# Attention ahead of two MLPs: the order of the work set step by step on four engines

## The chip, the cores and the metric

The kernel runs on one core of a Trainium2 chip. The metric is the device time of one execution in microseconds. The kernel before was run three times on its own and once under the hardware profiler. "Span" is the profiled stretch from its first to its last instruction, and all positions below ("at 33.67") are microseconds from its start.

## The reference

A soft-capped attention over 2 batches and 12 heads (448 tokens, 64 columns per head) feeds a relu-squared MLP, and that feeds a SoLU MLP. The change touches the first part and its seam to the second.

```python
def _attn_ref(q, k, v, cap):
    scale = 1.0 / np.sqrt(q.shape[-1])
    scores = scale * np.matmul(q, k.transpose(0, 1, 3, 2))
    scores = cap * np.tanh(scores / cap)
    scores = scores - np.max(scores, axis=-1, keepdims=True)
    attn = np.exp(scores)
    attn = attn / (np.sum(attn, axis=-1, keepdims=True) + 1e-09)
    return np.matmul(attn, v).astype(np.float32)

x = attn_out.transpose(0, 2, 1, 3).reshape(896, 768)
h = x @ w_in                       # 768 x 2048
r = np.maximum(h, 0.0)
y = (s * (r * r) + b) @ w_out      # then the SoLU MLP on y
```

## The kernel before

**Tiling.** The attention works on twelve head pairs, called n = 0 to 11 here; a pair is two heads of one batch. Products of full precision are made of three matmuls over split operands (a high and a low part: `kh`, `kl`, `qh`, `ql`, `xh`, `xl`). The maximum is not searched for, since the cap bounds the scores. An input-dependent branch chooses between two arms; the arm that runs here is the one without `general`, whose tiles are laid out by key.

**The steps of a pair.**

- `prep(n)`: TensorE (PE) transposes k and q into the PSUM tiles `pk` and `pq` (L412). VectorE (DVE) makes `kh`, `kl` and `ql` (L431, L432, L424), ScalarE (ACT) makes `qh` (L423).
- `scores_by_key(n, c)`, c = 0 to 3: PE writes a score tile `s` (L450), ACT reads it with a tanh into the tile `e` (L455). Two score tiles exist, so a score step waits for the tanh of the step before the last.
- `exps_by_key(n)`: ACT takes the exponential of `e` in two halves (L462). GpSimd (POOL) adds the tiles of `e` into `c` in two steps (L467, L468, 2.1 us each), and DVE closes the sum with two short instructions (L471).
- `products_by_key(n, half)`: PE multiplies `e` with v into the PSUM tile `o`, eight matmuls each half (L483).
- `values_by_key(n)`: PE spreads the sums into the PSUM tile `m` (L497). DVE turns that (`mt`, L504), takes the reciprocal (`few`, L506), spreads it (`rs`, L510) and scales `o` to `xf` (L515). POOL splits `xf` into `xh` and `xl` (L520, L524).

The PSUM tiles `pk`, `pq`, `o` and `m` of all pairs share four slots. A slot can be written again when its reader is done: `kl` for `pk`, `ql` for `pq`, `xf` for `o`, `mt` for `m`.

**The order.** The loop below is the whole attention. `on_pe` fixes only the order on PE: each step comes behind the last PE instruction of the step ahead. The order on DVE, ACT and POOL is the scheduler's. Iteration n runs scores of pair n, products and sums of pair n-2 and prep of pair n+2. The first half of the products stands between score steps 1 and 2, the second half behind step 3.

**The weights.** The first MLP's weight blocks `wi0`, `wi1`, ... arrive as 64-bit numbers in two raw tiles and are converted in seven operations (`convert`, L218 to 250: ACT L223, DVE L224, L228, L233, L237, ACT L243, DVE L244). `weights.pump(1)` runs one step of that; before, one step stands behind each pair from iteration 3 on, and a raw tile is loaded again when its block is converted. MLP matmuls of block `wi0` (L327 to L329, tile `in`) start on PE while the last pair's products are still to be done.

**The start.** Fourteen small matmuls on `ones` (L169, tile `idle`) run ahead of everything on PE. POOL's queue holds the loads of q for three groups, memsets of the unused parts of each loaded tile, three small loads (`s_t`, `b_t`, `g_t`, L160) and the identity matrix. On DVE four tiny operations on `b_t` (L742, L743) stand ahead of the first `kh`.

Of the kernel before, what the change touches and what calls it, by code (L numbers as in the profile page):

```python
# [37 lines left out]
def tile_softcap_attention__relu2__solu(  # L38
# [50 lines left out]

    def load_by_key(t, src, b, heads, by_pair=False, odd=None):  # L90

        n_heads = heads.stop - heads.start
        for par in range(2):
            fours, threes = (slice(0, D), slice(D, P))[::1 - 2 * par]
            lo = 4 * D if par == 0 else 3 * D
            toks = (slice(0, lo), slice(lo, S))[::1 - 2 * par]
            queue = odd if odd and par else nc.sync
            for rows, tok, n in ((fours, toks[0], 4), (threes, toks[1], 3)):  # L100
                part = src[b, heads.start + par:heads.stop:2, tok]
                if by_pair:
                    for pr in range(n_heads // 2):
                        queue.dma_start(
                            out=t[rows, pr, :n, par],
                            in_=part[pr].rearrange("(p c) d -> p c d", c=n),
                        )
# [5 lines left out]
            if by_pair:  # L113
                nc.gpsimd.memset(t[threes, :, 3:, par], 0.0)
            else:
                nc.gpsimd.memset(t[threes, par:n_heads:2, 3 * D:], 0.0)
            yield
# [15 lines left out]
    nc.scalar.dma_start(out=cap_t, in_=cap.partition_broadcast(P))  # L133
    load_by_query(first["q"][:, 1:], q, 0, slice(2, 4), nc.gpsimd)
    for pr in range(2):
        pair = slice(2 * pr, 2 * pr + 2)
        odd = nc.scalar if pr == 0 else nc.sync
        for _ in load_by_key(first["k"][:, pr:pr + 1], k, 0, pair, by_pair=True, odd=odd):
            pass
# [6 lines left out]
    ident = cst.tile([P, P], F32, name="ident")  # L146
    make_identity(nc, ident)
# [8 lines left out]
    for t, src in (  # L156
        (s_t, s_in.partition_broadcast(P)), (b_t, b_in.partition_broadcast(P)),
        (g_t, g_ln.rearrange("(k p) -> p k", p=P)),
    ):
        nc.gpsimd.dma_start(out=t, in_=src)  # L160
# [5 lines left out]
    with psum("ps_w", 1) as ps_w:  # L166
        idle = ps_w.tile([P, 512], F32, name="idle")
        for n in range(14):
            nc.tensor.matmul(idle[:D, :D], lhsT=ones, rhs=ones, start=True, stop=True)  # L169
# [14 lines left out]
    def layers(ctx, general):  # L184
# [33 lines left out]
        def convert(wt, raw, n, h, l, g=None):  # L218
# [4 lines left out]
            nc.scalar.activation(out=w, in_=hi.bitcast(F32), func=AF.Abs)  # L223
# [18 lines left out]
            if g is None:  # L242
                nc.scalar.copy(out=h, in_=w)  # L243
# [8 lines left out]
        class Weights:  # L252
# [31 lines left out]
            def job(self, n):  # L284
                self.load(n + 1)
                name, _, dst, g, _ = self.jobs[n]
                h, l = dst()
                raw, cnt = self.raw.pop(n)
                yield from convert(self.wt_of(f"wt_{name}"), raw, cnt, h, l, g)
                self.parts[name] = h, l  # L290
                self.done += 1
# [82 lines left out]
        nat = {}  # L374

        def load_group(g, names=("k", "q", "v")):
            b, i = divmod(g, GB)
            heads = slice(4 * i, 4 * i + 4)
            for nm, src in (("k", k), ("q", q), ("v", v)):
# [7 lines left out]
                shape = [P, 2, NC, 2, D] if by_pair else [P, 4, NC * D]  # L387
                t = ap_.tile(shape, F32, tag=f"{nm}n", name=f"{nm}n{g}", bufs=3)
                if by_key:
                    for _ in load_by_key(t, src, b, heads, by_pair):  # L390
                        pass
                elif by_pair:
# [10 lines left out]
        def prep(n):  # L403
# [3 lines left out]
            for nm in ("k", "q"):  # L407
# [3 lines left out]
                for c in range(NC):  # L411
                    turn = nc.tensor.transpose(  # L412
# [3 lines left out]
                st["pe"] = turn  # L416
# [5 lines left out]
                if nm == "q":  # L422
                    nc.scalar.mul(out=hi, in_=ps, mul=sc_t)  # L423
# [19 lines left out]
        def scores_by_key(n, c):  # L443
# [4 lines left out]
            for x, (kk, qq) in enumerate(terms(n)):  # L448
                for j, rows in enumerate(both):
                    st["pe"] = nc.tensor.matmul(  # L450
# [4 lines left out]
            st["act"] = nc.scalar.activation(  # L455
# [3 lines left out]
        def exps_by_key(n):  # L459
            e = st["e", n]  # L460
            for tiles in (slice(0, 4), slice(4, 7)):
                nc.scalar.activation(  # L462
                    out=e[:, tiles, :], in_=e[:, tiles, :], func=AF.Exp, scale=a_t, bias=a_t
                )
            c = ap_.tile([P, 2, S], F32, tag="c", name=f"c{n}", bufs=2)
            st["c", n] = c
            nc.gpsimd.tensor_tensor(out=c, in0=e[:, 0:2, :], in1=e[:, 2:4, :], op=ALU.add)  # L467
# [8 lines left out]
        def products_by_key(n, half):  # L476
# [4 lines left out]
            for c in (2 * half, 2 * half + 1):  # L481
                for j in range(2):
                    st["pe"] = nc.tensor.matmul(  # L483
# [6 lines left out]
        def values_by_key(n):  # L490
            b, i_p = divmod(n, NPAIR)
            if n == 0:
                xs["x"] = act_tiles("x")
            tok = slice(b * S, (b + 1) * S)
            m = ps_t.tile([P, 512], F32, tag="t", name=f"m{n}")
            for j in range(2):
                st["pe"] = nc.tensor.matmul(  # L497
# [17 lines left out]
            st["dve"] = nc.vector.tensor_tensor(  # L515
                out=xf, in0=st["o", n][:, :S], in1=r, op=ALU.mult
            )
# [147 lines left out]

        def g_tile(fc, name):
# [7 lines left out]
        load_group(2, ("k", "q"))  # L674
        load_group(1, ("v",))
# [27 lines left out]
        else:  # L703
            def on_pe(step, *args):

                with tc.issue_after(st["pe"].ins):
                    step(*args)

            prep_half(1)
            prep_half(1)  # L710
            weights.load(1)
            load_group(2, ("v",))
            for n in range(NPR + 2):
                now, last = n < NPR, n >= 2
                for c in range(NC):
                    if now:
                        on_pe(scores_by_key, n, c)
                    if c == 1:
                        if 0 <= n - 1 < NPR:
                            exps_by_key(n - 1)  # L720
                        if last:
                            on_pe(products_by_key, n - 2, 0)
                if last:
                    on_pe(products_by_key, n - 2, 1)
                on_pe(prep_half, n + 2)
                on_pe(prep_half, n + 2)
                if last:
                    on_pe(values_by_key, n - 2)
                    with tc.issue_after(st["dve"].ins), tc.issue_after(st["act"].ins):
                        weights.pump((n > 2) if now else 3)  # L730
                if n % 2 == 1 and n // 2 + 3 < NG:
                    load_group(n // 2 + 3)
# [3 lines left out]
        for n in range(GSB):  # L736
# [3 lines left out]
            if n % 2 == 0:  # L740
                behind = slice(M0, M0 + 2)
                nc.vector.tensor_copy(gh[:, behind], b_t.to_broadcast([P, 2]))  # L742
                nc.vector.tensor_tensor(  # L743
                    out=gl[:, behind], in0=b_t.to_broadcast([P, 2]), in1=full(gh[:, behind]),
# [299 lines left out]
```

## Time and profile before

| what | value |
|---|---|
| three runs | 476.80, 477.12, 477.62 us; median 477.12 us |
| the profiled execution | 478.09 us, of which its span is 476.3 us |
| PE busy | 463.2 us, 97% of the span |
| DVE, ACT, POOL busy | 351.8, 275.9, 95.6 us |
| the chain that ended last | PE 95% |
| attention on PE | from 6.31 us; first MLP matmul at 109.15 us |
| one pair in the steady part | 8.22 us, at positions 33.67, 41.89, ..., 91.21 |

The profiled execution is 1.79 us longer than its span and 0.97 us longer than the median of the three runs. A row of a timeline gives start, busy time, engine, line, operation, tile written <- tiles read, and, in brackets, how long the engine sat idle ahead of it and what ended that. Neighbours in a PE timeline overlap (a matmul's end is modelled), so the price of a step is the distance of its start from the start of the next step, not the busy time.

### The profile page before, as it was taken

What the parts mean: (1) busy time and instruction counts of PE and PEld (TensorE: products, weight loads), DVE (VectorE), ACT (ScalarE), POOL (GpSimd) and SP (SyncE); (2) the same over time, 40 slices, a digit from 0 to 9 for tenths busy, and PEclk for the clock granted to TensorE, in tenths of its full rate; (3) what the DMA queues carried; (4) which work ended last, traced back from release to release, by engine and by line L of the source; (5) the groups of instructions that cost most, each with busy time, mean ns of one, the idle gap of its engine ahead of it and who ended that gap; (6) DMA issues with size and microseconds to landing.
All of it is one profiled execution on the core that took longest, in us unless ns stands there. A gap on an engine that the chain in (4) does not pass through costs nothing.

```text
span 476.3 us, 6578 instructions
## 1 busy us (share of the span) xinstructions
PE 463.2 (97%) x2412; PEld 376.9 (79%) x2412; DVE 351.8 (74%) x566; ACT 275.9 (58%) x398; POOL 95.6 (20%) x103
## 2 busy tenths in 40 slices
PE   6799999999999999999999999999999999999995
PEld 5554544445998998988988889989888898999894
DVE  3358999999888899996699988998958984043110
ACT  2989788881666678775677746555625452033120
POOL 8648788894000000000000000000001010000000
PEclk9889999999999999999999999999999999999998
DMA  6885514001546577643223324443311300011112
GB/s 141 162 217 117 129 29 106 0 1 40 194 140 201 180 221 218 198 134 88 61 78 112 105 89 133 131 126 142 135 66 67 132 1 23 11 33 34 34 41 66
DMA packets 43416, 49.28 MB, mean 103 GB/s; under 512 B 20016, under 2 KB 35504, under 8 KB 43376
## 3 DMA queue, kind: packets, MB, share of 16 engines
q1 hardware_dynamic: 41712, 47.39, 34.2%
q0 software_dynamic: 576, 1.15, 1.1%
q8 instruction: 21, 0.34, 0.3%
q10 hardware_dynamic: 1088, 0.23, 0.2%
q14 instruction: 19, 0.16, 0.1%
HBM read 46.01 MB, written 2.75 MB: 102 GB/s over the span
## 4 chain that ended last, share of the span: by engine, by line
PE 95%; ACT 2%; DMA 2%; DVE 0%; SPq 0%; issue 0%
PE in L328 8%; PE o L483 8%; PE in L327 8%; PE y L329 8%; PE y L328 8%; PE y L327 8%; PE in L329 8%; PE s L450 7%; PE h L914 4%; PE h L918 4%; PE h L922 4%; PE o L964 4%; PE o L965 4%; PE o L963 4%; PE m L497 2%; DMA raw<-in_k_dram 2%
## 5 line engine op out<-in xcount | busy, mean ns | idle before, releaser
L328 PE MATMUL in<-xl,h_wi 128*128 128x510 f32 (+2 forms) x192 | 70.0, 365 | 0.0
L327 PE MATMUL in<-xh,h_wi 128*128 128x510 f32 (+2 forms) x192 | 69.8, 365 | 0.0
L329 PE MATMUL in<-xh,l_wi 128*128 128x510 f32 (+2 forms) x192 | 69.6, 364 | 0.0
L899 POOL TENSOR_SCALAR va<-vs 128x1 f32<-128x1 f32 x7 | 2.0, 286 | 321.3 <-ACT e L898 321.3
L359 ACT ACTIVATE gh<-g,s_t 128x510 fp32r<-128x510 f32 (+1 forms) x64 | 42.2, 668 | 19.0 <-PE y L329 19.0
L360 DVE SCALAR_TENSOR_TENSOR gl<-g,s_t,gh 128x510 fp32r<-128x510 f32 (+1 forms) x64 | 42.8, 682 | 3.1 <-ACT gh L359 3.0
L455 ACT ACTIVATE e<-s 128x896 f32<-128x896 f32 (+1 forms) x48 | 36.6, 813 | 8.9 <-PE s L450 6.0
L462 ACT ACTIVATE e<-e,a_t 128x1792 f32<-128x1792 f32 (+1 forms) x24 | 40.8, 1698 | 0.6
L483 PE MATMUL o<-e,vn 128*64 128x448 f32 x192 | 40.9, 550 | 0.0
L328 PEld LDWEIGHTS in<-xl,h_wi 128*128 128x128 f32 x192 | 36.0, 188 | 5.0 <-issue 1.4
L327 PEld LDWEIGHTS in<-xh,h_wi 128*128 128x128 f32 x192 | 36.0, 188 | 4.3 <-issue 0.7
L329 PEld LDWEIGHTS in<-xh,l_wi 128*128 128x128 f32 x192 | 36.0, 188 | 3.6
L963 PE MATMUL o<-w2o_h,lh 128*128 128x384 f32 (+1 forms) x104 | 35.6, 342 | 0.5 <-ACT lh L205 0.5
L965 PE MATMUL o<-w2o_h,ll 128*128 128x384 f32 (+1 forms) x104 | 35.4, 342 | 0.0
L964 PE MATMUL o<-w2o_l,lh 128*128 128x384 f32 (+1 forms) x104 | 35.4, 340 | 0.0
L914 PE MATMUL h<-w2i_h,yh 128*128 128x512 f32 x84 | 33.0, 393 | 0.0
L918 PE MATMUL h<-w2i_l,yh 128*128 128x512 f32 x84 | 33.0, 392 | 0.0
L922 PE MATMUL h<-w2i_h,yl 128*128 128x512 f32 x84 | 32.8, 390 | 0.0
L471 DVE SCALAR_TENSOR_TENSOR c<-c,e 64x448 f32<-64x448 f32 x24 | 26.5, 1102 | 7.2 <-POOL c L468 6.8
L467 POOL TENSOR_TENSOR c<-e 128x896 f32<-128x896 f32 x12 | 25.3, 2108 | 17.4 <-PE m L497 8.7
L205 ACT CAST lh<-x 128x512 fp32r<-128x512 f32 x14 | 7.5, 590 | 35.7 <-PE o L964 35.6
L223 ACT ACTIVATE wt_wi<-raw 128x768 f32<-128x768 f32 x16 | 14.6, 912 | 22.7 <-DMA raw<-in_moe_w_in_dram 12.7
(424 smaller groups left out, 1120.7 us busy)
## 6 DMA issues: line engine op xcount, KB each, us to landing
raw<-in_moe_w_in_dram SPq DMA_DIRECT2D x16, 768.0 KB, 4.9
raw<-in_moe_w_out_dram SPq DMA_DIRECT2D x24, 512.0 KB, 3.6
raw_w2i<-in_moe_w_in_dram SPq DMA_DIRECT2D x12, 512.0 KB, 4.8
raw<-in_moe_w_out_dram SPq DMA_DIRECT2D x8, 768.0 KB, 4.2
vn<-in_v_dram SPq DMA_DIRECT2D x12, 128.0 KB, 3.7
qn<-in_q_dram SPq DMA_DIRECT2D x12, 112.0 KB, 2.8
kn<-in_k_dram SPq DMA_DIRECT2D x20, 64.0 KB, 3.0
vn<-in_v_dram SPq DMA_DIRECT2D x12, 96.0 KB, 3.4
```

The costliest lines, as they stand in the source:

```text
L327: nc.tensor.matmul(o, lhsT=wh, rhs=xh, start=first, stop=False)
L328: nc.tensor.matmul(o, lhsT=wh, rhs=xl, start=False, stop=False)
L329: nc.tensor.matmul(o, lhsT=wl, rhs=xh, start=False, stop=last)
L359: nc.scalar.mul(out=gh[:, :m], in_=r2, mul=s_t)
L360: nc.vector.scalar_tensor_tensor(out=gl[:, :m], in0=r2, scalar=s_t, in1=full(gh[:, :m]), op0=ALU.mult, op1=ALU.subtract,)
L483: st["pe"] = nc.tensor.matmul(o[j * D:(j + 1) * D, :S], lhsT=vn[:, 2 * (n % 2) + j, c * D:(c + 1) * D], rhs=st["e", n][:, 2 * c + j if c < ...
L914: nc.tensor.matmul(ps[:, n, :], lhsT=yh[:, kk, :], rhs=big["w2i_h"][:, kk, f], start=(kk == 0), stop=False,)
L918: nc.tensor.matmul(ps[:, n, :], lhsT=yh[:, kk, :], rhs=big["w2i_l"][:, kk, f], start=False, stop=False,)
L922: nc.tensor.matmul(ps[:, n, :], lhsT=yl[:, kk, :], rhs=big["w2i_h"][:, kk, f], start=False, stop=(kk == KD - 1),)
L963: nc.tensor.matmul(o, lhsT=lh[:, f, :], rhs=wh, start=(f == 0), stop=False)
L964: nc.tensor.matmul(o, lhsT=lh[:, f, :], rhs=wl, start=False, stop=False)
L965: nc.tensor.matmul(o, lhsT=ll[:, f, :], rhs=wh, start=False, stop=(f == KF2 - 1))
```

## The change

The order is now fixed on PE, DVE, ACT and POOL: `then` puts each step's first instruction on each engine behind that engine's last instruction of the steps ahead. The per-pair order is new, and so is the placing of the steps around it:

- iteration n: score steps 0 and 1 of pair n, both halves of the products of n-2, the sums of n-2, score steps 2 and 3, prep of n+2. The x split runs a pair later (`split_x(n-3)`).
- the exponential and the POOL sum of the first half of pair n stand ahead of score step 2; there are three `c` tiles instead of two.
- no conversion step in iterations 3 to 9. `wi0` is converted wholly on DVE: four DVE operations in iteration 1 and three in iteration 2. Iterations 10 to 13 hold 2, 3, 2 and 2 steps of the next blocks.
- `qh` of pairs 1 to 3 is made on DVE. Prep of pair 1 comes behind score steps 0 and 1 of pair 0.
- at the start: 18 matmuls on `ones` ahead of the branch and 6 more behind `pq0`; the identity is made ahead of the q loads; the three small loads come behind the q loads of group 2; the memsets are done once for each of three kept tiles per name; the operations on `b_t` are POOL's.

The core of the diff:

```diff
-        def exps_by_key(n):
+        def exps_by_key(n, half):
             e = st["e", n]
+            tiles = (slice(0, 4), slice(4, 7))[half]
+            nc.scalar.activation(
+                out=e[:, tiles, :], in_=e[:, tiles, :], func=AF.Exp, scale=a_t, bias=a_t
+            )
+
+        def sums_by_key(n, half):
+            e = st["e", n]
+            if half == 0:
+                c = ap_.tile([P, 2, S], F32, tag="c", name=f"c{n}", bufs=3)
+                st["c", n] = c
+                nc.gpsimd.tensor_tensor(out=c, in0=e[:, 0:2, :], in1=e[:, 2:4, :], op=ALU.add)
+                return
+            c = st["c", n]
             nc.gpsimd.tensor_tensor(out=c, in0=c, in1=e[:, 4:6, :], op=ALU.add)
...
-                nc.scalar.activation(out=w, in_=hi.bitcast(F32), func=AF.Abs)
+            if early:
+                nc.vector.tensor_scalar(
+                    out=wb, in0=hi, scalar1=0x7FFFFFFF, scalar2=None, op0=ALU.bitwise_and
+                )
+            else:
+                nc.scalar.activation(out=w, in_=hi.bitcast(F32), func=AF.Abs)
...
-            def on_pe(step, *args):
-                with tc.issue_after(st["pe"].ins):
+            def then(step, *args):
+                with ExitStack() as behind:
+                    for ins in last.values():
+                        behind.enter_context(tc.issue_after(ins))
+                    n = len(traced)
                     step(*args)
+                for ins in traced[n:]:
+                    if ins.engine in ordered:
+                        last[ins.engine] = ins
+            for n in range(6):
+                nc.tensor.matmul(idle[:D, :D], lhsT=ones, rhs=ones, start=True, stop=True)
+            then(scores_by_key, 0, 0)
+            then(scores_by_key, 0, 1)
+            then(prep_half, 1)
+            then(prep_half, 1)
+            weights.load(0)
+            load_group(2, ("k", "q"))
+            load_small()
...
+            steps = {1: 3, 2: 2, NPR - 2: 2, NPR - 1: 3}
             for n in range(NPR + 2):
+                now = n < NPR
+                if now and n > 0:
+                    then(scores_by_key, n, 0)
+                    then(scores_by_key, n, 1)
+                if not now:
+                    then(weights.pump, 2)
+                if n >= 2:
+                    then(products_by_key, n - 2, 0)
+                    then(products_by_key, n - 2, 1)
+                    then(values_by_key, n - 2)
+                if now:
+                    then(exps_by_key, n, 0)
+                if n >= NPR:
+                    then(split_x, n - 2)
+                elif n >= 3:
+                    then(split_x, n - 3)
+                if now:
+                    then(sums_by_key, n, 0)
+                    then(scores_by_key, n, 2)
+                    then(scores_by_key, n, 3)
+                    then(exps_by_key, n, 1)
+                then(prep_half, n + 2)
+                then(prep_half, n + 2)
+                then(weights.pump, steps.get(n, 0))
+                if now:
+                    then(sums_by_key, n, 1)
```

On PE, iteration 3 from its second score step on. The number behind a letter is the pair (`s3_1` is score step 1 of pair 3), the last number only tells tiles apart. Before:

```order
L450 MATMUL s3_1_451<-qh3_336,kl3_328 128x448 x2
L483 MATMUL o1_466<-e1_285,vn0_180 64x448 x4
L450 MATMUL s3_2_471<-qh3_336,kh3_327 128x448 x2
L450 MATMUL s3_2_471<-ql3_337,kh3_327 128x448 x2
L450 MATMUL s3_2_471<-qh3_336,kl3_328 128x448 x2
L450 MATMUL s3_3_479<-qh3_336,kh3_327 128x448
L450 MATMUL s3_3_479<-ql3_337,kh3_327 128x448
L450 MATMUL s3_3_479<-qh3_336,kl3_328 128x448
L483 MATMUL o1_466<-e1_285,vn0_180 64x448 x4
L412 MATMUL pk5_488<-ident_78,kn2_187 128x128 x4
L412 MATMUL pq5_497<-ident_78,qn2_198 128x112 x4
L497 MATMUL m1_506<-c1_382,ones_90 64x448 x2
```

The same place on PE now:

```order
L468 MATMUL s3_1_468<-qh3_351,kl3_343 128x448 x2
L507 MATMUL o1_476<-e1_303,vn0_179 64x448 x8
L517 MATMUL m1_485<-c1_321,ones_88 64x448 x2
L468 MATMUL s3_2_501<-qh3_351,kh3_342 128x448 x2
L468 MATMUL s3_2_501<-ql3_352,kh3_342 128x448 x2
L468 MATMUL s3_2_501<-qh3_351,kl3_343 128x448 x2
L468 MATMUL s3_3_509<-qh3_351,kh3_342 128x448
L468 MATMUL s3_3_509<-ql3_352,kh3_342 128x448
L468 MATMUL s3_3_509<-qh3_351,kl3_343 128x448
L426 MATMUL pk5_515<-ident_62,kn2_231 128x128 x4
L426 MATMUL pq5_524<-ident_62,qn2_242 128x112 x4
```

The products are one piece, and the sums `m1` moved from behind the prep to right behind the products. In the program as built, `o1` is written into the slot that `m0` held, so it waits for `mt0`; `o2` waits for `mt1` in the same way.

On DVE, from the end of pair 3's prep to `xf0`. Before:

```order
L424 SCALAR_TENSOR_TENSOR ql3_337<-pq3_331,sc_t_87,qh3_336 128x448
L471 SCALAR_TENSOR_TENSOR c1_382<-c1_382,e1_285 64x448 x2
L431 CAST kh4_414<-pk4_409 128x512
L432 TENSOR_TENSOR kl4_415<-pk4_409,kh4_414 128x512
L504 STREAM_TRANSPOSE mt0_432<-m0_429 128x448
L424 SCALAR_TENSOR_TENSOR ql4_424<-pq4_418,sc_t_87,qh4_423 128x448
L506 RECIPROCAL few0_434<-mt0_432 128x14
L510 STREAM_TRANSPOSE rs0_436<-few0_434 128x448
L515 TENSOR_TENSOR xf0_438<-o0_387,rs0_436 128x448
```

The same stretch on DVE now:

```order
L442 SCALAR_TENSOR_TENSOR ql3_352<-pq3_346,sc_t_85,qh3_351 128x448
L222 TENSOR_SCALAR wt_wi0_357<-raw0_58 128x768
L227 TENSOR_SCALAR wt_wi0_357<-wt_wi0_357 128x768
L231 TENSOR_SCALAR wt_wi0_357<-wt_wi0_357 128x768
L236 SCALAR_TENSOR_TENSOR wt_wi0_357<-raw0_58,wt_wi0_357 128x768
L495 SCALAR_TENSOR_TENSOR c1_321<-c1_321,e1_303 64x448 x2
L524 STREAM_TRANSPOSE mt0_410<-m0_407 128x448
L526 RECIPROCAL few0_412<-mt0_410 128x14
L530 STREAM_TRANSPOSE rs0_414<-few0_412 128x448
L535 TENSOR_TENSOR xf0_416<-o0_398,rs0_414 128x448
```

Four operations of the conversion of `wi0` now stand ahead of the closing of `c1` and of `mt0`. A pair later the same happens with three:

```order
L442 SCALAR_TENSOR_TENSOR ql4_450<-pq4_444,sc_t_85,qh4_449 128x448
L240 SCALAR_TENSOR_TENSOR wt_wi0_357<-raw0_58,wt_wi0_357 128x768
L247 CAST h_wi0_355<-wt_wi0_357 128x768
L250 TENSOR_TENSOR l_wi0_356<-wt_wi0_357,h_wi0_355 128x768
L495 SCALAR_TENSOR_TENSOR c2_419<-c2_419,e2_381 64x448 x2
L524 STREAM_TRANSPOSE mt1_488<-m1_485 128x448
```

From iteration 3 on DVE's list holds no conversion until iteration 10.

## Rows read from the trace of the kernel before

**Rows 1.** The page's head: busy time, share of the span and instructions by engine.

```profile
PE 463.2 (97%) x2412; PEld 376.9 (79%) x2412; DVE 351.8 (74%) x566; ACT 275.9 (58%) x398; POOL 95.6 (20%) x103
```

**Rows 2.** Windows: stretch, length, busy PE PEld DVE ACT POOL, granted clock, DMA, GB/s.

```profile
20.00:26.00 6.00, 5.71 (x23) 4.50 (x25) 3.27 (x6) 5.32 (x7) 3.62 (x4) 0.50 0.57 149
...
40.00:110.00 70.00, 70.00 (x414) 33.87 (x413) 67.63 (x82) 58.69 (x60) 58.72 (x44) 1.00 0.23 56
```

**Rows 3.** Timeline of PE, from pair 0's first score to pair 3's.

```profile
10.96 0.74 PE L450 MATMUL s<-qh,kh 64*128 64x448 f32 x2
...
13.46 0.47 PE L450 MATMUL s<-qh,kh 64*128 64x448 f32 x2 [0.24 <-ACT e L455]
...
14.97 0.60 PE L412 MATMUL pk<-ident,kn 128*128 128x128 f32 x4
...
16.98 0.47 PE L450 MATMUL s<-qh,kh 64*128 64x448 f32 x2 [1.03 <-ACT e L455]
...
20.29 0.74 PE L450 MATMUL s<-qh,kh 64*128 64x448 f32 x2 [1.81 <-ACT e L455]
...
33.67 0.48 PE L450 MATMUL s<-qh,kh 64*128 64x448 f32 x2
```

**Rows 4.** Timeline of PE, one steady pair: the first row of each step.

```profile
58.33 0.48 PE L450 MATMUL s<-qh,kh 64*128 64x448 f32 x2
...
59.77 1.72 PE L483 MATMUL o<-e,vn 128*64 128x448 f32 x8
61.42 0.47 PE L450 MATMUL s<-qh,kh 64*128 64x448 f32 x2
...
63.02 1.72 PE L483 MATMUL o<-e,vn 128*64 128x448 f32 x8
64.68 0.66 PE L412 MATMUL pk<-ident,kn 128*128 128x128 f32 x4
...
65.65 0.97 PE L497 MATMUL m<-c,ones 128*64 128x448 f32 x4
66.55 0.48 PE L450 MATMUL s<-qh,kh 64*128 64x448 f32 x2
```

**Rows 5.** Timeline of PE at the seam to the MLP.

```profile
105.29 3.18 PE L483 MATMUL o<-e,vn 128*64 128x448 f32 x16
108.30 0.92 PE L497 MATMUL m<-c,ones 128*64 128x448 f32 x4
109.15 0.47 PE L327 MATMUL in<-xh,h_wi 128*128 128x448 f32 x1
```

**Rows 6.** Timeline of ACT, pair 0 and the first tanh of pair 1.

```profile
12.49 1.73 ACT L455 ACTIVATE e<-s 128x896 f32<-128x896 f32 x2 [0.79 <-PE s L450]
...
18.82 0.61 ACT L423 ACTIVATE qh<-pq,sc_t 128x448 fp32r<-128x448 f32 x1
19.33 1.71 ACT L455 ACTIVATE e<-s 128x896 f32<-128x896 f32 x2
```

**Rows 7.** Timeline of DVE: start, a closing sum alone, a `mt`, two conversions.

```profile
8.71 0.24 DVE L742 CAST gh<-b_t 128x2 fp32r<-128x2 f32 x2 [4.81 <-DMA b_t<-in_moe_b_dram]
...
21.17 1.27 DVE L471 SCALAR_TENSOR_TENSOR c<-c,e 64x448 f32<-64x448 f32 x2 [1.02 <-POOL c L468]
...
42.07 0.64 DVE L504 STREAM_TRANSPOSE mt<-m 128x448 f32<-128x448 f32 x1
...
44.68 2.23 DVE L224 TENSOR_SCALAR wt_wi<-wt_wi 128x768 f32<-128x768 f32 x1
...
114.83 0.95 DVE L237 SCALAR_TENSOR_TENSOR wt_wi<-raw,wt_wi 128x768 uint32<-128x768 uint32 x1
...
119.80 0.55 DVE L224 TENSOR_SCALAR wt_wi<-wt_wi 128x768 f32<-128x768 f32 x1
```

**Rows 8.** Timeline of POOL: the two sums of pair 3.

```profile
42.17 2.12 POOL L467 TENSOR_TENSOR c<-e 128x896 f32<-128x896 f32 x1 [0.94 <-PE m L497]
44.37 2.12 POOL L468 TENSOR_TENSOR c<-c,e 128x896 f32<-128x896 f32 x1
```

More of the change, by code (lines that the diff above doesn't have):

```diff
@@ L137, in tile_softcap_attention__relu2__solu @@
         odd = nc.scalar if pr == 0 else nc.sync
-        for _ in load_by_key(first["k"][:, pr:pr + 1], k, 0, pair, by_pair=True, odd=odd):
-            pass
+        load_by_key(first["k"][:, pr:pr + 1], k, 0, pair, by_pair=True, odd=odd)
         if pr == 0:
@@ L167, in tile_softcap_attention__relu2__solu @@
         idle = ps_w.tile([P, 512], F32, name="idle")
-        for n in range(14):
+        for n in range(18):
             nc.tensor.matmul(idle[:D, :D], lhsT=ones, rhs=ones, start=True, stop=True)
@@ L288, in job @@
                 raw, cnt = self.raw.pop(n)
-                yield from convert(self.wt_of(f"wt_{name}"), raw, cnt, h, l, g)
+                yield from convert(
+                    self.wt_of(f"wt_{name}"), raw, cnt, h, l, g, name == "wi0" and not general
+                )
                 self.parts[name] = h, l
@@ L374, in layers @@
         nat = {}
+        kept = {}
         def load_group(g, names=("k", "q", "v")):
@@ L422, in prep @@
                 if nm == "q":
-                    nc.scalar.mul(out=hi, in_=ps, mul=sc_t)
+                    if n in (1, 2, 3) and not general:
+                        nc.vector.tensor_scalar(
+                            out=hi, in0=ps, scalar1=sc_t, scalar2=None, op0=ALU.mult
+                        )
+                    else:
+                        nc.scalar.mul(out=hi, in_=ps, mul=sc_t)
                     nc.vector.scalar_tensor_tensor(
@@ L664, in layers, with load_small @@
             add_w2out(f)
+        def load_small():
+            for t, src in (
+                (s_t, s_in.partition_broadcast(P)), (b_t, b_in.partition_broadcast(P)),
+                (g_t, g_ln.rearrange("(k p) -> p k", p=P)),
+            ):
+                nc.gpsimd.dma_start(out=t, in_=src)
         def g_tile(fc, name):
@@ new lines, in layers @@
+            ordered = [e.engine for e in (nc.tensor, nc.vector, nc.scalar, nc.gpsimd)]
+            xs["x"] = act_tiles("x")
+            idle = ps_t.tile([P, 512], F32, tag="t", name="idle2")
+            for n in range(6):
[5 more added lines that the diff above has]
+            weights.load(0)
+            load_group(2, ("k", "q"))
@@ L711, in layers @@
+            load_small()
+            load_group(1, ("v",))
+            load_group(2, ("v",))
             weights.load(1)
-            load_group(2, ("v",))
+            steps = {1: 3, 2: 2, NPR - 2: 2, NPR - 1: 3}
             for n in range(NPR + 2):
[L714 to L730, printed above, removed]
+                now = n < NPR
[24 more added lines that the diff above has]
+                    then(sums_by_key, n, 1)
+                if n == NPR - 1:
+                    then(split_x, n - 2)
@@ L740, in layers @@
             if n % 2 == 0:
[L741 to L744, printed above, removed]
+                ends = slice(M0, M0 + 2)
+                nc.gpsimd.tensor_copy(gh[:, ends], b_t.to_broadcast([P, 2]))
+                nc.gpsimd.tensor_tensor(
+                    out=gl[:, ends], in0=b_t.to_broadcast([P, 2]), in1=full(gh[:, ends]),
                     op=ALU.subtract,
```

86 lines of the change are left out of this document (43 added, 43 removed).

## The prediction

> **What bounds the kernel now.** I read the page's head first: PE is busy 97% of the span [rows 1]. The windows then say where it is not, or is slow: from 40 to 110 PE has 70.00 of 70.00 us at a granted clock of 1.00, and from 20 to 26 it is busy 5.71 of 6.00 at 0.50, the 1.2 GHz level of its two (1.2 and 2.4) [rows 2]. So after the start only less time per matmul can help, and at the start there is idle time and a low clock to win. The timeline of PE shows the start: it waits for a tanh for 0.24, 1.03 and 1.81 us, and the stretch at half clock comes right behind the last two waits [rows 3]. In the same table of windows DVE stands at 67.63 of 70, next to full, and POOL at 58.72 [rows 2]. That fits the view of single rows: a conversion that takes 0.55 alone took 2.23 at 44.68, ending just behind a POOL sum that ran from 44.37 to 46.49 [rows 7, 8]. So a DVE operation of this kind and a POOL sum do not run at once: the later one waits for the whole of the earlier. Since this is where my forecast is decided, the Trainium skill is weighed on it further down.
>
> **Part 1: a steady pair.** The new order makes the same matmuls, with fewer changes between kinds. Step by step before, by distances of starts [rows 4]: scores 0 and 1 1.44 (58.33 to 59.77), half a product 1.65, scores 2 and 3 1.60, the other half 1.66, prep 0.97, sums 0.90; together 8.22. Now: scores 1.44; both halves in one piece 3.01 (105.29 to 108.30 is such a piece, [rows 5]); sums behind products 0.85 [rows 5]; scores 2 and 3 with a prep behind them 1.51 (13.46 to 14.97, [rows 3]); prep 0.97. Sum 7.78, a gain of 0.44 per pair. Were only the products' joint won, it would be 0.30; 0.50 if the prep also shrinks to the 0.92 that the changes of kind around it leave room for by my estimate. Seven pairs (3 to 9) have no other load: 7 x 0.44 = 3.1 (2.1 to 3.5). Pairs 10 and 11 have no prep and conversions again: 0.4 together (0 to 0.9). What must keep up: ACT takes 6.84 per pair (12.49 to 19.33, [rows 6]), so 0.94 of 7.78 is its cover; POOL has two sums of 2.2 and a split, 58.72 of 70 us for 8.5 pairs, 6.9 per pair, so its cover is 0.9; DVE loses its conversion, up to 2.23 a pair, so its cover grows. I take nothing for these; if one is late, the pair falls back to 7.8 to 8.2, which is in the bounds. The split a pair later only matters for when `xf` comes free, at no cost.
>
> **Part 2: the start.** Before, DVE stood 4.81 us on the load of `b_t` until 8.71 and made `kh0` behind that [rows 7]; now nothing stands ahead of `kh0`, and prep of pair 1 stands behind the first two score steps. I estimate the first score about 1.0 earlier than 10.96 [rows 3]. Then ACT: of its 6.84 per pair 0.51 is `qh` (18.82 to 19.33, [rows 6]), which DVE now makes for pairs 1 to 3. Three pairs of 6.33 from a first tanh at 11.5 end at 30.5, one `qh4` later 31.0. The first score of pair 3 can stand a microsecond ahead of its tanh, so at 30.0 at best, 3.7 earlier than 33.67 [rows 3]. At worst only the 1.0 remains. I take 2.9 (1.0 to 3.7), near the upper end, since PE's own waits of 3.08 are for ACT [rows 3] and ACT is what is relieved; the pair's 0.44 of iteration 2 is within it. The ten extra small matmuls lie in time in which PE waits; the small loads delay POOL's first sum by some tenths, and `m0` is far from needing that; the memsets done once spare POOL 0.45 now and then. These I take at nothing. The first load of weights moves ahead in SP's queue and pushes the loads of pair 4 and of later v behind it; they have a whole pair of time.
>
> So the order alone would bring 2.9 + 3.1 + 0.4 = 6.4 (3.1 to 8.1).
>
> **Part 3: the conversion in iterations 1 and 2.** This is what the change adds. Its seven DVE operations now stand in front of the sums of c1 and c2, and behind these wait `mt0` and `mt1`, for which PE's `o1` and `o2` wait (their PSUM slot). Behind `o1` on PE waits everything: `m1`, the next scores, ACT after them. The sum for `o1`: PE wants it 1.44 behind pair 3's first score, at 30.8 + 1.44 = 32.2. DVE has four conversion operations (0.55 + 0.55 + 0.55 + 0.95), the closing sums 1.27 and `mt` 0.64: 4.51 [rows 7]. By my estimate it begins at 27.0, when POOL's second sum of pair 1 has ended. With no further POOL sum between, `mt0` is done at 31.5 and PE does not wait. Each POOL sum that gets between adds 2.12 [rows 8]: one gives 33.6, a wait of 1.4; two give 35.7, a wait of 3.5. The two sums of pair 2 become ready in just this stretch, the first surely inside the conversion, the second when the closing sums are due, within half a microsecond. At `o2` it is the same with 0.95 + 0.55 + 0.95 + 1.27 + 0.64 = 4.36 and pair 3's sums: 0 to 4.6. A long wait at one place moves all later work apart, and then the other is mostly short. I take one long wait of 4.0 and one short of 0.8: +4.8 (0 to 9). For the seam, where conversions of iterations 10 to 13 stand near the last sums, I add 0.3 (0 to 1.0).
>
> The Trainium skill bears on the price of a sum between. Its page "SBUF — State Buffer" (section on the doors to SBUF) says that the two engines' shared port pair is an exclusive lock, held for a whole instruction, and not a split of bandwidth. By the lock two sums cost 4.2; by a split, in which both only run slower, the stretch would end some 2 us earlier and the whole would come out near 474. The 2.23 us row, which ends with the POOL sum and not later by a share of it, is on the lock's side [rows 7, 8].
>
> **The sum.** -6.4 + 4.8 + 0.3 = -1.3. Against the profiled execution, 478.09, that is 476.8. That execution is 0.97 above the median of the three runs; on the median's scale the forecast is 475.8.
>
> **The rivals.** *B, the sums keep out of the way.* If POOL's sums come a little later or earlier than I think, both waits are 0 to 1.4: -6.4 + 0.7 + 0.3 = -5.4, at 471.7 (470.2 to 473). For it: the decision hangs on half a microsecond. Against it: the first sum of pair 2 falls into the conversion by any estimate that I could make.
>
> *C, both waits are long, and it is slower.* Two waits of 4.0 each: -6.4 + 8.0 + 0.3 = +1.9, at 479.0. PE's waits of 1.03 and 1.81 were followed by six microseconds at 1.2 GHz [rows 2, 3], which is 3 us of work lost; a wait of 4 may bring that again, to 482. It decides for slower from a total wait of 6.1. For it: both places have the same make. Against it: after a long wait at `o1` the second place has more room. The skill's page "TensorE: Matmul & The Clock Gate" (Part 1) calls the lower clock the default, which activity lifts and idling brings back; by that rule C is the dearer kind, 482; the rows agree in that the half clock stands behind waits, and no row here shows a wait of 4.
>
> *D, one of the other engines is late in every pair.* With ACT's or POOL's cover of 0.9 used up by hand-overs, the 0.44 per pair is gone: -3.3 + 4.8 + 0.3 = +1.8, at 478.9. Against it: in 8.22 they have kept up without a single wait of PE. That the order is not what the code says can be left out: the order of the built program is as listed.
>
> **How the numbers follow.** Forecast (A) 0.42, B 0.27, C 0.22, D 0.09. A alone reaches from 473.3 to 477.8. For a fall or rise that counts I take 0.2%, about 1 us, which is what a measurement of this kernel can tell from no change. Of A 0.26 lies below 476.2, 0.11 within 1 us of 477.12 and 0.05 above; B is all below; of C and D together 0.05 is within, 0.26 above. So faster 0.53, same 0.16, slower 0.31. The range from 470.9 to 480.5 leaves out the far end of B (0.08) and the clock's part of C (0.1).
>
> **What would show it.** Pair 3's first score at 30 to 31; PE idle ahead of `o` in iterations 3 and 4, ended by DVE's `mt`, with two POOL sums inside DVE's conversion and closing sums; then starts of pairs 7.78 apart; a granted clock of 1.00 from there to the end. I am wrong in the first step if pair 3 starts later than 32.7, in part 1 if pairs are 8 apart, and in part 3 if PE does not wait for `mt`, or waits at both places. A low granted clock behind such a wait would be C.

## The result and the profile after

The changed kernel takes 480.58 us in the median of eight runs (478.20 to 481.76), the kernel before 477.19 in the median of eight (476.80 to 478.22). The ratio is 1.0061, with an interval of 1.0037 to 1.0086: slower by 0.6%, where 475.8 was forecast. The profiled execution is the longest of the eight, 481.76, with a span of 479.9; that of the kernel before was a long one too (478.09, span 476.3), so the spans differ by 3.6 where the medians differ by 3.4. Line numbers below are those of the changed kernel: products L507, sums L517, `mt` L524, closing sums L495, POOL's sums L489 and L492, the MLP's matmuls L335 to L337.

What PE waited for, whole run of the changed kernel (us in total, times, longest):

```profile
PE o L507 <- DVE mt L524: 4.1, 2, 3.7
PE pk L426 <- DMA kn<-in_k_dram: 1.9, 1, 1.9
...
PE in L335 <- ACT g L353: 1.2, 1, 1.2
```

These three waits are new. The windows of the changed kernel, columns as in [rows 2]:

```profile
10.00:20.00 10.00, 8.03 (x49) 5.66 (x47) 5.92 (x9) 8.16 (x8) 8.92 (x14) 0.83 1.19 185
20.00:26.00 6.00, 4.95 (x35) 3.23 (x35) 5.06 (x9) 5.93 (x7) 3.24 (x2) 1.00 0.90 169
...
40.00:110.00 70.00, 66.10 (x390) 34.28 (x388) 59.46 (x79) 55.48 (x57) 53.67 (x33) 0.95 0.23 57
...
44.00:50.00 6.00, 6.00 (x18) 2.59 (x20) 5.87 (x8) 0.22 (x1) 4.20 (x3) 0.55 0.53 119
```

From 40 to 110, where PE had been busy throughout, it now idles 3.90 us and the granted clock is 0.95 in the mean; from 44 to 50 it is 0.55. The timeline of PE in the changed kernel shows where, beside [rows 3, 4]:

```profile
15.04 0.94 PE L426 MATMUL pk<-ident,kn 128*128 128x128 f32 x4 [1.88 <-DMA kn<-in_k_dram]
...
30.55 0.47 PE L468 MATMUL s<-qh,kh 64*128 64x448 f32 x2
...
32.44 3.23 PE L507 MATMUL o<-e,vn 128*64 128x448 f32 x16 [0.40 <-DVE mt L524]
...
43.97 5.94 PE L507 MATMUL o<-e,vn 128*64 128x448 f32 x16 [3.69 <-DVE mt L524]
49.71 0.95 PE L517 MATMUL m<-c,ones 128*64 128x448 f32 x4
...
53.03 0.47 PE L468 MATMUL s<-qh,kh 64*128 64x448 f32 x2
...
60.78 0.47 PE L468 MATMUL s<-qh,kh 64*128 64x448 f32 x2
```

Pair 3 starts at 30.55, 3.12 ahead of the kernel before. `o1` waits 0.40. `o2` waits 3.69, and the sixteen matmuls behind that wait take 5.74 (43.97 to 49.71) where such a piece took 3.01 [rows 5]: about half pace, 2.7 us more. From pair 5 on pairs stand 7.75 apart (53.03 to 60.78) instead of 8.22.

What `mt` waited for stands in DVE's and POOL's timelines of the changed kernel. DVE:

```profile
25.26 2.35 DVE L231 TENSOR_SCALAR wt_wi<-wt_wi 128x768 uint32<-128x768 uint32 x1
...
28.52 3.18 DVE L495 SCALAR_TENSOR_TENSOR c<-c,e 64x448 f32<-64x448 f32 x2
31.73 0.65 DVE L524 STREAM_TRANSPOSE mt<-m 128x448 f32<-128x448 f32 x1
...
36.81 2.35 DVE L247 CAST h_wi<-wt_wi 128x768 fp32r<-128x768 f32 x1
...
40.07 3.17 DVE L495 SCALAR_TENSOR_TENSOR c<-c,e 64x448 f32<-64x448 f32 x2
43.27 0.65 DVE L524 STREAM_TRANSPOSE mt<-m 128x448 f32<-128x448 f32 x1
```

POOL:

```profile
24.86 2.32 POOL L492 TENSOR_TENSOR c<-c,e 128x896 f32<-128x896 f32 x1 [0.74 <-ACT e L480]
28.32 2.25 POOL L489 TENSOR_TENSOR c<-e 128x896 f32<-128x896 f32 x1 [1.14 <-ACT e L480]
...
36.06 2.68 POOL L489 TENSOR_TENSOR c<-e 128x896 f32<-128x896 f32 x1
40.68 2.07 POOL L492 TENSOR_TENSOR c<-c,e 128x896 f32<-128x896 f32 x1 [1.94 <-ACT e L480]
```

L231, which takes 0.56 at 131.63 where POOL is idle, lasts 2.35 here and ends 0.43 behind the sum of 24.86; the closing sums, 1.27 alone [rows 7], last 3.18 beside the sum of 28.32. A pair later the same two delays come from the sums of 36.06 and 40.68. The conversion had begun at 24.08, so the sum of 24.86 inside it is still the second of pair 1, and that of 28.32 the first of pair 2; at the second place both sums are pair 3's. The Trainium skill, "SBUF — State Buffer" (section "SBUF: two separate sides"), has the port pair held for a whole instruction; these rows agree, since each delayed operation ends only behind the sum.

The seam on PE in the changed kernel, beside [rows 5]:

```profile
115.66 0.97 PE L517 MATMUL m<-c,ones 128*64 128x448 f32 x2
116.56 0.48 PE L337 MATMUL in<-xh,l_wi 128*128 128x448 f32 x1
...
116.96 0.96 PE L517 MATMUL m<-c,ones 128*64 128x448 f32 x2
117.86 0.47 PE L335 MATMUL in<-xh,h_wi 128*128 128x448 f32 x1
...
131.49 0.47 PE L335 MATMUL in<-xh,h_wi 128*128 128x448 f32 x1 [1.21 <-ACT g L353]
```

The sums of pair 11 are cut in two by a matmul of the MLP and take 0.90 each half, where a whole set takes 0.85 [rows 5]. Later PE waits for ACT, and ACT's timeline of the changed kernel says why:

```profile
130.12 0.89 ACT L226 ACTIVATE wt_wi<-raw 128x768 f32<-128x768 f32 x1 [3.61 <-DMA raw<-in_moe_w_in_dram]
130.90 0.97 ACT L353 ACTIVATE g<-in 128x448 f32<-128x448 f32 x2
```

An operation on a raw weight block that had not landed stood ahead of `g` in ACT's queue.

The balance by positions, of the two profiled executions:

| PE starts | before | after | after minus before |
|---|---|---|---|
| pair 3 | 33.67 | 30.55 | -3.12 |
| pair 5 | 50.11 | 53.03 | +2.92 |
| pair 10 | 91.21 | 91.79 | +0.58 |
| pair 11 | 98.31 | 99.01 | +0.70 |
| second layer (first `y`) | 230.4 | 233.6 | +3.2 |
| end of span | 476.3 | 479.9 | +3.6 |

Between pairs 3 and 5 6.04 us are lost (waits of 4.09 and half pace of 2.7, less two pairs' gain of 0.47 each, make 5.85 of it), 2.34 come back in five pairs, and 2.5 are lost between pair 11 and the second layer.

### The profile page after: what moved, and what is told of

It reads as the page before. It is cut to its first block, busy times and chain, and to the rows that moved or that the text cites. A ratio compares the mean times of both kernels' runs of the same rounds, so it can differ in the third digit from the quotient of the medians.

```text
span 479.9 us, 6593 instructions
## 1 busy us (share of the span) xinstructions
PE 462.2 (96%) x2432; PEld 379.4 (79%) x2432; DVE 354.5 (74%) x567; ACT 272.2 (57%) x393; POOL 95.3 (20%) x95
## 4 chain that ended last, share of the span: by engine, by line
PE 83%; DVE 8%; DMA 3%; SPq 3%; issue 1%; ACT 1%; DVEq 0%; ACTq 0%
PE y L337 8%; PE y L336 8%; PE y L335 8%; PE in L335 7%; PE in L337 7%; PE in L336 7%; PE o L507 5%; PE s L468 4%; PE h L980 4%; PE h L984 4%; PE h L988 4%; PE o L1030 4%; PE o L1029 4%; PE o L1031 4%; DVE c L495 2%; SPq L112 2%
## 5 line engine op out<-in xcount | busy, mean ns | idle before, releaser
L335 PE MATMUL in<-xh,h_wi 128*128 128x510 f32 (+2 forms) x192 | 70.1, 366 | 1.2 <-ACT g L353 1.2
L337 PE MATMUL in<-xh,l_wi 128*128 128x510 f32 (+2 forms) x192 | 69.9, 365 | 0.0
L507 PE MATMUL o<-e,vn 128*64 128x448 f32 x192 | 41.6, 576 | 4.1 <-DVE mt L524 4.1
L335 PEld LDWEIGHTS in<-xh,h_wi 128*128 128x128 f32 x192 | 36.0, 187 | 6.6 <-ACT g L353 1.6
L337 PEld LDWEIGHTS in<-xh,l_wi 128*128 128x128 f32 x192 | 36.0, 188 | 4.3 <-issue 0.7
L495 DVE SCALAR_TENSOR_TENSOR c<-c,e 64x448 f32<-64x448 f32 x24 | 29.8, 1240 | 7.3 <-POOL c L492 6.9
L507 PEld LDWEIGHTS o<-e,vn 128*64 128x64 f32 x192 | 13.9, 144 | 25.9 <-issue 18.9
L489 POOL TENSOR_TENSOR c<-e 128x896 f32<-128x896 f32 x12 | 29.1, 2423 | 4.0 <-ACT e L480 3.8
L492 POOL TENSOR_TENSOR c<-c,e 128x896 f32<-128x896 f32 x12 | 25.7, 2140 | 16.4 <-ACT e L480 16.3
```

Of the source, the lines that this page charges most:

```text
L335: nc.tensor.matmul(o, lhsT=wh, rhs=xh, start=first, stop=False)
L337: nc.tensor.matmul(o, lhsT=wl, rhs=xh, start=False, stop=last)
L507: nc.tensor.matmul(o[j * D:(j + 1) * D, :S], lhsT=vn[:, 2 * (n % 2) + j, c * D:(c + 1) * D], rhs=st["e", n][:, 2 * c + j if c < 3 else 6, ...
```

## The experiments

The theory for them: TensorE's order is worth what was forecast, and is lost again in two places, by the conversion ahead of `mt` and at the seam. Ratios are to the kernel before, on the same chip; e7, e8 and e10 were executed once each, so their times settle little and their traces are what is read.

**e1_spread: the conversion back where it was, one step behind each pair.**

```diff
-            steps = {1: 3, 2: 2, NPR - 2: 2, NPR - 1: 3}
+            steps = {n: 1 for n in range(3, NPR)}
...
-                    then(weights.pump, 2)
+                    then(weights.pump, 3)
...
-                    self.wt_of(f"wt_{name}"), raw, cnt, h, l, g, name == "wi0" and not general
+                    self.wt_of(f"wt_{name}"), raw, cnt, h, l, g, False
```

> The changed kernel with the conversions placed as before: one step behind each pair from iteration 3 on, three in each of the last two iterations, none in iterations 1 and 2, with ScalarE's two operations of the block again on ScalarE. All the rest of the change stays. Theory (the conversion ahead of the closing sums makes TensorE wait at o1 and o2, and the clock falls behind the longer wait): no wait of TensorE for mt, granted clock 1.00 from 20 us on, pair 5 starts at about 46 where the changed kernel had it at 53.03, pairs stay 7.75 apart, and the time is about 474 (472.5 to 475.5). Rival 1 (the order cannot carry a conversion per pair: DVE is late for mt again, pair after pair): pairs 8.2 or more apart and 477 or more. Rival 2 (o waits for mt because of the slot, with or without a conversion): the waits at o1 and o2 stay, 480.

Measured: 476.44 (474.56 to 477.76), ratio 0.9978 (0.9959 to 0.9998). Timeline of PE in e1_spread:

```profile
28.73 0.47 PE L468 MATMUL s<-qh,kh 64*128 64x448 f32 x2
...
52.06 0.48 PE L468 MATMUL s<-qh,kh 64*128 64x448 f32 x2
...
90.40 0.47 PE L468 MATMUL s<-qh,kh 64*128 64x448 f32 x2 [0.21 <-ACT e L473]
...
123.12 0.68 PE L335 MATMUL in<-xh,h_wi 128*128 128x448 f32 x2 [2.68 <-ACT xh L203]
```

No wait for `mt` is left, pair 5 starts at 44.28, pair 6 at 52.06, and pair 11 at 90.40: 8.6 us ahead of the changed kernel, 7.9 ahead of the kernel before. Both rivals fall: the pairs stand 7.78 apart with a conversion in each. But the second layer starts at 228.4, only 2.0 ahead of before. The end of the attention came early, and then PE waited 2.68 us. DVE and ACT in e1_spread:

```profile
118.64 0.62 DVE L535 TENSOR_TENSOR xf<-o,rs 128x448 f32<-128x448 f32 x1
...
121.72 0.89 ACT L226 ACTIVATE wt_wi<-raw 128x768 f32<-128x768 f32 x1 [5.35 <-DMA raw<-in_moe_w_in_dram]
122.51 0.55 ACT L203 CAST xh<-xf 128x448 fp32r<-128x448 f32 x1
```

The split of pair 11, which PE needs, had its `xf` at 119.26 and ran at 122.51, 3.25 later: ahead of it in ACT's queue stood an operation on a raw block, for whose load ACT sat idle 5.35 us. The granted clock fell right behind PE's wait, in e1_spread's window:

```profile
125.00:130.00 5.00, 5.00 (x20) 4.45 (x20) 4.18 (x7) 4.96 (x10) 0.00 (x0) 0.73 0.58 179
```

So the gain is real and most of it was given back at the seam, which the forecast of 474 had not seen. Four of the ten executions, at a mean granted clock of 0.996 and 0.997, took 474.56 to 475.33, the other six, at 0.986 to 0.994, 476.38 to 477.76; that the fall of the clock behind this wait makes the difference is likely and not shown, since only one of the ten was traced.

**e2_pe_order_alone: the kernel before with TensorE's order of a pair alone.**

```diff
                         if last:
                             on_pe(products_by_key, n - 2, 0)
-                if last:
-                    on_pe(products_by_key, n - 2, 1)
+                            on_pe(products_by_key, n - 2, 1)
+                            on_pe(values_by_key, n - 2)
                 on_pe(prep_half, n + 2)
                 on_pe(prep_half, n + 2)
                 if last:
-                    on_pe(values_by_key, n - 2)
                     with tc.issue_after(st["dve"].ins), tc.issue_after(st["act"].ins):
```

> The kernel before with one part of the change alone: TensorE's order of a pair (both halves of the products and the sums behind score step 1), all else as before, the other engines' order the scheduler's. Theory of the prediction's part 1 (0.44 us per pair come from TensorE's order alone): pairs 7.78 apart and 473 to 474. Rival (the sums now stand earlier on TensorE, and DVE and GpSimd, whose order is not brought along, deliver c and mt too late): TensorE waits in several pairs ahead of o or m, 480 to 487.

Measured: 487.27, ratio 1.0225 (1.0203 to 1.0247). The rival holds. The waits of PE in e2_pe_order_alone:

```profile
PE o L483 <- DVE mt L504: 4.3, 3, 2.1
...
PE m L497 <- DVE c L471: 2.0, 1, 2.0
```

Pairs 3 to 8 do stand 7.75 apart (31.75, 39.50, 47.26, 55.01 and on to 70.52); then `mt` and the sums, whose order on POOL and DVE was not brought along, come late, and pair 9 starts at 82.24. To keep the 0.47 per pair to the end, the other engines' new order is needed too.

**e3_one_step_more: the changed kernel with one conversion step more, in iteration 9** (`steps` gets `9: 1`).

> The changed kernel with one conversion step more, in iteration 9. Theory on the seam (TensorE's 1.21 us wait for ScalarE's g in the first MLP comes from the weights being one step behind the kernel before at the end of the attention, with ScalarE's operation on a raw tile standing ahead of g): that wait goes, 1.0 to 1.5 less than the changed kernel, and the waits at o1 and o2 stay. Rival (the wait is set by the order of the seam, not by the number of steps): the wait stays and the time is the changed kernel's or up to 1 more, since the step stands ahead of a closing sum in iteration 9.

Measured: 479.88 (478.81 to 481.62). The wait for `g` is gone from the list of waits, a wait of 0.3 for `h_wi` is there, and the waits at `o1` and `o2` stay (0.94 and 3.70). The gain of 0.7 in the medians is less than the 1.0 to 1.5 expected and than the spread of either kernel, and the ratios to the kernel before are 1.0060 and 1.0061; the trace bears the theory out and the time does not settle it.

**e4_spread_k_by_pair: e1_spread with the k of pair 2 loaded ahead of that of pair 3.**

```diff
+                    if g == 1 and by_pair:
+                        for pr in range(2):
+                            pair = slice(heads.start + 2 * pr, heads.start + 2 * pr + 2)
+                            load_by_key(t[:, pr:pr + 1], src, b, pair, by_pair)
+                    else:
+                        load_by_key(t, src, b, heads, by_pair)
-                    load_by_key(t, src, b, heads, by_pair)
```

> The kernel of e1_spread with the eight loads of group 1's k ordered by pair, so that the four of pair 2 come first. Theory (the start lost 1.88 us at the transpose of pair 2's k, which waits for the last load of its group, and the clock fell behind that wait): the transpose of pair 2 starts at 13.2 instead of 15.04, the granted clock of 10 to 20 rises from 0.83 to over 0.9, pair 3's first score stands at 29 instead of 30.5, and the time is 1.0 to 1.7 less than e1_spread. Rival (ScalarE sets the start anyhow): pair 3 starts within 0.5 us of e1_spread's and the time is the same.

Measured: 476.45, ratio 0.9986 (0.9974 to 0.9998), as e1_spread. PE in e4_spread_k_by_pair:

```profile
12.97 0.60 PE L431 MATMUL pk<-ident,kn 128*128 128x128 f32 x4
...
17.27 0.48 PE L473 MATMUL s<-qh,kh 64*128 64x448 f32 x2 [1.30 <-ACT e L478]
...
28.57 0.47 PE L473 MATMUL s<-qh,kh 64*128 64x448 f32 x2
```

The transpose came 1.6 us earlier than in e1_spread (14.56), and pair 3 0.16 (28.73): a wait for a tanh took the place of the wait for k. The rival holds: with k early, ACT is what PE waits for.

**e5_hold_act_dve: e1_spread with the MLP's work on ACT and DVE held behind the attention's last instruction there.** `held` is the list of those two instructions.

```diff
-            for _ in in_unit(*((ps_a, "a") if n == 0 else (ps_b, "b")), tok, fc):
-                weights.pump(1)
-                side.pump(1)
+            unit = in_unit(*((ps_a, "a") if n == 0 else (ps_b, "b")), tok, fc)
+            more = True
+            while more:
+                with ExitStack() as behind:
+                    for ins in held:
+                        behind.enter_context(tc.issue_after(ins))
+                    more = next(unit, 0) != 0
+                    if more:
+                        weights.pump(1)
+                        side.pump(1)
```

> The kernel of e1_spread, and on ScalarE and VectorE nothing of the first MLP (conversions emitted there, g) is issued ahead of the last instruction of the attention. Theory (e1_spread was 7.9 us ahead of the kernel before at pair 11 and lost 6 of it at the seam, since ScalarE's queue held an operation that waits for a raw weight block ahead of the split of pair 11, for which TensorE waited 2.68 us, and the clock fell behind that): that wait goes, the granted clock stays 1.00, the second layer's first matmul (y) starts at 224 to 225 instead of 228.4, and the time is 472 to 473. Rival (the weights themselves are late, so the wait only moves to the first matmul of a later block): TensorE waits there for h_wi or l_wi and the time is 475.5 to 477.

Measured: 472.29 (471.57 to 472.82), ratio 0.9891 (0.9874 to 0.9907). PE waits nowhere between pair 11 and the second layer, and that starts at 224.6. First row of its `y` matmuls in e5_hold_act_dve (the two times behind the durations are first and last start):

```profile
L335 PE MATMUL y<-gh,h_wo0a x8: 335/364/399, 224.6 to 229.0; 128*128 128x512 f32 x4, 128*128 128x386 f32 x4
```

The theory holds: the order in the queues, not late weights, had taken the gain. ACT and DVE were held together; that it was ACT's queue is read from e1_spread's trace.

**e6_hold_all: as e5_hold_act_dve, with TensorE's last instruction in `held` too.**

> As e5_hold_act_dve, and on TensorE too: the first matmul of the MLP comes behind the sums of pair 11, so the products and the sums of that pair are one piece each. Theory (the pieces in which the products and sums of pair 11 were cut cost 1.3 us of TensorE): TensorE waits 0.3 to 1.3 us for the closing of c11 and saves 1.3, so 0 to 1.0 us less than e5_hold_act_dve, 471.5 to 473. Rival (the wait for c11 is as long as the cut was dear, or longer): the same or up to 1 us more than e5_hold_act_dve.

Measured: 471.90 (470.94 to 472.21), ratio 0.9890 (0.9874 to 0.9907). PE in e6_hold_all:

```profile
101.64 3.18 PE L507 MATMUL o<-e,vn 128*64 128x448 f32 x16
104.65 1.53 PE L517 MATMUL m<-c,ones 128*64 128x448 f32 x4
106.11 0.47 PE L335 MATMUL in<-xh,h_wi 128*128 128x448 f32 x1
```

Products and sums are whole, and the sums take 1.46 (104.65 to 106.11), 0.6 more than elsewhere. From pair 11 (90.88) to the second layer (222.9) are 132.0 us, as before the change (132.1), where the changed kernel took 134.6. Against e5_hold_act_dve the medians differ by 0.4, which the runs do not resolve. This version beats the kernel before by 1.1% and the changed kernel by about 1.7% (0.9890 against 1.0061).

**e7_qh_on_act: e1_spread with `qh` of pairs 1 to 3 on ACT** (`if n in (1, 2, 3) and not general` made false).

> The kernel of e1_spread with qh of pairs 1 to 3 on ScalarE as before. Theory (ScalarE sets the start, and each qh moved off it is worth its 0.51 us): pair 3's first score at 30.0 to 30.4 instead of 28.73. Rival (the loads and the earlier first score made the start, not the three operations): 28.6 to 29.2.

**e8_fewer_idle: e1_spread with 14 idle matmuls ahead of the branch and 1 behind `pq0`.**

> The kernel of e1_spread with 14 idle matmuls ahead of the branch as before and 1 instead of 6 behind pq0. Theory (the ten more let the clock rise before the first score): the score steps of pair 0 run at half pace (about 0.37 us per pair of matmuls instead of 0.20) until about 12, pair 3's first score 0.3 to 1.0 later than 28.73. Rival (the first score waits for other things and ScalarE sets the rest): the pace of pair 0 is lower, pair 3's start the same.

Measured: e7_qh_on_act 477.42, e8_fewer_idle 474.81. PE in e7_qh_on_act:

```profile
14.95 0.65 PE L426 MATMUL pk<-ident,kn 128*128 128x128 f32 x4 [1.94 <-DMA kn<-in_k_dram]
...
29.77 0.47 PE L468 MATMUL s<-qh,kh 64*128 64x448 f32 x2
```

PE in e8_fewer_idle:

```profile
8.99 0.74 PE L468 MATMUL s<-qh,kh 64*128 64x448 f32 x2 [0.37 <-ACT qh L441]
...
29.78 0.47 PE L468 MATMUL s<-qh,kh 64*128 64x448 f32 x2
```

In e8 the scores of pair 0 run at half pace (0.74 for a first row that lasts 0.47 else) and pair 3 starts 1.05 later than in e1_spread. But e5_hold_act_dve has the whole start of e1_spread, added idle matmuls and all, and does the same:

```profile
9.59 0.74 PE L468 MATMUL s<-qh,kh 64*128 64x448 f32 x2
...
29.98 0.47 PE L468 MATMUL s<-qh,kh 64*128 64x448 f32 x2
```

So one and the same start brings pair 3 anywhere from 28.73 to 29.98, and e8 does not show what the added idle matmuls are worth. e7 falls between its two forecasts and inside this spread; the k of pair 2 came late in it, as in the changed kernel, and the clock of 10 to 20 was 0.83 in both. What the moved `qh` are worth stays open.

**e10_first_place_only: the changed kernel with conversions in iteration 1 alone, two single steps in 4 and 6** (`steps` is `{1: 3, 4: 1, 6: 1, ...}`).

> The changed kernel with the conversion of wi0 on VectorE left in iteration 1 only (four operations ahead of the closing of c1 and of mt0); its other two steps stand alone in iterations 4 and 6, nothing in iteration 2. Theory (each place makes its own wait, and a place without a conversion has none): a wait of TensorE at o1 of 0.3 to 4, none at o2, pair 5 at 47 to 50 instead of 53.03, and behind the single steps waits at o4 and o6 of 0 to 1.5. Rival (o2 waits for mt1 whatever stands ahead, since VectorE has fallen behind by then): the wait at o2 stays at 2 or more.

Measured: 475.0. PE in e10_first_place_only:

```profile
31.61 3.23 PE L507 MATMUL o<-e,vn 128*64 128x448 f32 x16 [1.25 <-DVE mt L524]
...
39.39 3.23 PE L507 MATMUL o<-e,vn 128*64 128x448 f32 x16
...
45.72 0.47 PE L468 MATMUL s<-qh,kh 64*128 64x448 f32 x2
```

`o1` waits 1.25, `o2` not at all, pair 5 starts at 45.72 (ahead of the 47 to 50 expected), the granted clock stays 1.00 from 20 to 120, and the only other wait for `mt` is 0.71 in iteration 7. Each place makes its own wait, and the second is the dear one: from pair 3 (28.88) to pair 5 are 16.84 us, 5.64 less than in the changed kernel, where the wait at `o2` and the half pace behind it were 6.4 and `o1` waited 0.85 less.

**e11_hold_only: the changed kernel with the hold of e6_hold_all, the conversion left in iterations 1 and 2.**

> The changed kernel with the seam of e6_hold_all alone (nothing of the first MLP is issued on TensorE, VectorE and ScalarE ahead of the attention's last instruction there); the conversion of wi0 stays in iterations 1 and 2. Theory (the two losses are separate: about 4 us of waits at o1 and o2 and up to 3 us of clock behind them, and about 2.5 us at the seam): the waits at o1 and o2 stay, the 1.21 us wait for g and the cut pieces go, 1.5 to 2.5 less than the changed kernel, 478 to 479. Rival (the seam costs only a kernel that arrives early, as e1_spread did): the time stays at 480 or more.

Measured: 480.28 (477.78 to 481.04), ratio 1.0056 (1.0039 to 1.0074), as the changed kernel. PE in e11_hold_only:

```profile
43.83 4.99 PE L507 MATMUL o<-e,vn 128*64 128x448 f32 x16 [3.69 <-DMA kn<-in_k_dram]
48.59 0.99 PE L517 MATMUL m<-c,ones 128*64 128x448 f32 x4
...
113.33 1.62 PE L517 MATMUL m<-c,ones 128*64 128x448 f32 x4 [1.35 <-DVE c L495]
```

The waits at `o1` (0.96) and `o2` (3.69) stay; the profile puts the second down to a load, but `mt1` ended at 43.78, right ahead of it. The wait for `g` is gone, but PE waits 1.35 for the closing of `c11`, ahead of which three conversion operations of iteration 11 stand on DVE, and from pair 11 (98.06) to the second layer (232.0) only 0.7 is saved. The rival is borne out: with the conversions of the change the hold brings nothing that the runs resolve, and with those of e1_spread it brings 4.2 to 4.5 (472.29 and 471.90 against 476.44).

## Why the prediction was wrong

**Part 1, the pair: right.** 7.78 was forecast, 7.75 measured. e2 adds what I had not said: on the kernel before, TensorE's order alone costs 2.2%.

**Part 2, the start: the size came out in part by luck.** 2.9 was forecast for pair 3, 3.12 measured. The first score came 2.4 earlier, not 1.0, and most of that was lost again at 15.04 to the load of pair 2's k, whose queue I had passed over. e4 shows that without this wait PE waits for ACT instead. The other executions with the same start reach pair 3 at 28.73 to 29.98 (e1, e3, e5, e6, e10, e11), 3.7 to 4.9 ahead of the kernel before, so the term was rather too small. What the moved `qh` and the added idle matmuls have in it no run shows.

**Part 3, the waits for `mt`: right in mechanism, and in size as a sum.** One long and one short wait of together 4.8 were forecast, 3.69 and 0.40 measured, each place with two POOL sums beside DVE's conversion and closing sums. At `o1` the parts were off and made up for each other: two sums were to make a wait of 3.5 from a start at 27.0, but DVE began at 24.08, pair 1's second sum got in as well, and PE waited 0.40. The sign "or waits at both places" did not fit a forecast of two waits. e1 shows that without the conversions there both waits go, e10 that the second goes with its own.

**The sum: two terms failed.** First, I charged the long wait with its own length and left the clock to rival C. The half pace behind `o2` cost 2.7; behind the same wait the piece took 6.03 in e3 and 4.76 in e11, 3.0 and 1.75 more than 3.01. [Rows 2, 3] had already shown half clock behind waits half as long; it belonged into the forecast itself. Not every wait is followed by it: behind 1.21 for `g`, 1.25 in e10 and 1.35 in e11 the granted clock stayed at 1.00. That the wait is what lowered the clock is argued from its place in each trace (the changed kernel, e1, e2, e3, e11) and from e10, where without the wait at `o2` the clock stays up; a wait with the clock kept up was not tried. In the eight executions time goes with the clock: the two shortest (478.20 and 478.67) have a mean granted clock of 0.994, two of the longest (481.37 and 481.76) one of 0.986 and 0.985. But e11 took 480.77 at 0.995 and 480.38 at 0.986, and the kernel before 477.08 at 0.995 and 477.00 at 0.985, so the mean clock does not explain the spread. The Trainium skill's page "TensorE: Matmul & The Clock Gate" (Part 1) says that an idle engine goes back to the lower clock. The 0.55 behind the wait at `o2` agrees.

Second, the seam, taken at 0.3 (0 to 1.0), cost 2.5: 1.21 for `g`, 0.9 for the sums cut in two, and 0.4 that I did not assign beyond 0.1 for the cut products. I had priced the conversions there as if only DVE were at stake; the traces show the order that the scheduler made on ACT and PE around them as well. In e11, with this order mended, PE waits 1.35 for `c11` behind DVE's conversions, and only 0.7 of the 2.5 comes back. The 0.4 for pairs 10 and 11 did not come either: pair 10 took 7.22 (91.79 to 99.01) against 7.10.

Together, in the two profiled executions: 3.12 + 7 x 0.47 = 6.4 gained, 4.09 + 2.7 + 2.5 + 0.4 behind the second layer's start = 9.7 lost, 3.3 of the 3.6 in the spans. Rival C was the nearest in kind, with one long wait instead of two; B and D did not come.

## What to carry to other kernels

A gain ahead of a seam is worth only what the queues behind the seam let through: e1_spread was 7.9 us ahead and kept 2, and holding the next stage's work behind the last instruction of this one returned 4; where that last instruction itself was late (e11), the hold returned nothing that the runs resolve. Work that fills a gap on one engine is to be placed by what stands behind it in that queue, and by the other engine's operations that delay it, not by the engine's idle time. A long wait of TensorE is to be priced with the half-pace work that may follow it: 1.75 to 3.0 us behind 3.7 here.

## What was not expected of the hardware

POOL pays too: its first sum of a pair, 2.11 us in the mean of twelve before, lasts 2.42 in the changed kernel. From pair 5 on it takes 2.48 to 2.50 and begins each time while DVE's closing sums run (at 58.62, for example, with these from 56.67 to 59.14). And cutting a set of sums is dear: its four matmuls take 0.85 in one piece and took 1.80 with one matmul of the MLP between them.
